# Products with v in threes directly ahead of scores, one queue at both ends, own places for six score blocks

## The chip, the cores and the metric

The kernel runs on one core of a Trainium2 chip. Such a core has five engines, each with its own instruction stream: TensorE (PE) multiplies matrices, VectorE (DVE), ScalarE (ACT) and GpSimd (POOL) work on elements, and SyncE (SP) issues most of the transfers (DMA). They wait for one another by semaphores. The metric is the time of one execution on the device, in microseconds (us); smaller is better.

## The reference

Two batches of 12 heads, 448 positions, head size 64, pass through attention with mixed heads, then through two mixing networks, all in float32:

```python
scores = scale * np.matmul(q, k.transpose(0, 1, 3, 2))
scores = np.einsum('bhij,hg->bgij', scores, w_pre)     # mixes the heads
attn = softmax(scores)                                 # row by row
attn = np.einsum('bhij,hg->bgij', attn, w_post)        # mixes the heads again
x = np.matmul(attn, v)                                 # to (batch, position, 768)
h = np.maximum(xt @ w_tok1, 0.0) @ w_tok2              # over positions, xt = x transposed
u = x + h transposed
x = u + np.maximum(u @ w_ch1, 0.0) @ w_ch2             # over channels
# then a gated network: gelu(x @ w_in), halves u and v, v normalised and mixed
# over positions, out = x + (u * v) @ w_out
```

## The kernel before

Attention works on chunks of queries: 120, 120, 120 and 88 of the 448 of a batch (`CH`, line 48), eight chunks in all. For a chunk, `qk` (line 348) multiplies queries and keys for a pair of heads at a time; the two heads lie in the two halves of the partitions, so that each matmul uses 64 rows of the array and two run side by side. In the first batch a product is taken in float32, in the second in three products of parts (high times high, high times low, low times high). The scores of a chunk are copied to SBUF, tile `S`, heads beside positions.

Ten queries of a chunk with their 12 heads make a block of 120 partitions. A block is a DMA from `S` to a tile `P` (`b_dma`, line 382), so that heads come to lie on partitions and can be mixed by a matmul. There are 90 blocks: 12, 12, 12 and 9 for the chunks of a batch. The loop at line 568 takes one step for each, and every step works at several distances: it starts the DMA of block i + 8 (`LD`), splits block i + 6 (`LS`) into a high part `Ph` on ACT and a low part `Pl` on POOL or DVE, mixes heads and takes the exponential of block i + 4 (`b_pre`, `LP`), and normalises. For block i itself `b_post` mixes the heads again in four matmuls, and `b_turn` copies that to the tile `AT` of its chunk, on DVE, one step later. A pre is three matmuls (lines 412 to 414), a post is four (line 445, eight instructions). Both use the whole array.

Two more kinds of work stand between these steps. Scores of the chunk after next come in three steps of every chunk, two pairs of heads in each, by a table `extra` from step to work (lines 535 to 553). `av` (line 456) multiplies a finished chunk's `AT` with v for one pair of heads; its outputs are 64 columns wide, and two run side by side. When av is due is told by `av_due` (line 557): up to the last step with scores (`LAST`, step 70) three in step 2 and three in step 6 of a chunk of 12 blocks (3 and 7 of a chunk of 9), later two at a time. The banks of PSUM for scores and av come from one pool of three (`psA`); every second pair of scores takes one of its two from `psC`.

Tiles `P` come from a ring of `NP_BUFS` = 4; the first two blocks have places of their own among the tiles for the keys of the second batch. The engines run their instructions in the order in which the program writes them (line 987).

From step 71 on the weights of the later networks are loaded, and converted by a generator of steps on ACT, DVE and POOL: `pump(n)` (line 175) runs n of them, `rounds(n, w)` (line 188) runs waiting follow-up work n times and w conversion steps with each.

Of the kernel before, what the change touches and what calls it, by code (L numbers as in the profile page):

```python
# [8 lines left out]
F32 = mybir.dt.float32  # L9
# [21 lines left out]
def tile_kernel(ctx, tc, q, k, v, w_pre, w_post, w_tok1, w_tok2, w_ch1, w_ch2,  # L31
                w_u, w_v, g_ln, w_sg, b_sg, w_out, out):
    nc = tc.nc
    B, D, H, S = 2, 64, 12, 448
    P = 128
    R = 4
    KP = S // R
    NP = H // 2
    C = H * D
    NCC = C // P  # L40
# [5 lines left out]
    IB = 10  # L46
    BW = IB * H
# [18 lines left out]
    xT = xpool.tile([P, NCC, T], F32, name="xT")  # L66
# [108 lines left out]
    def pump(n):  # L175

        for _ in range(n):
            if wstate["conv"] < wstate["room"]:
                next(wstate["steps"], None)
# [8 lines left out]
    def rounds(n, w=1):  # L188

        for _ in range(n):  # L190
            for c in list(chains):
                if next(c, chains) is chains:
                    chains.remove(c)
            pump(w)
# [48 lines left out]
    for n, w in enumerate(chw):  # L243
        p_ch.append(piece(w, P, NCC, P))
        if n in V_EARLY:
            j = V_EARLY[n]
# [3 lines left out]
    for o in GATE_ORDER.split():  # L250
        j = int(o[1])
# [94 lines left out]
    SS = {}  # L346
# [34 lines left out]

    def b_dma(i):
        b, c, j, (r0, stp, m) = blocks[i]
        if i < 2:

            t = qp.tile([P, S], F32, tag=f"KH{NP - 1 - i}", name=f"P{i}")[:BW]
        else:
            t = ap_.tile([BW, S], F32, tag="P", name=f"P{i}", bufs=NP_BUFS)
        src = SS[b, c][r0:r0 + (m - 1) * stp + 1:stp]
        if i == 0:  # L390

            for eng, r in ((nc.sync, slice(0, IB // 2)), (nc.scalar, slice(IB // 2, IB))):
                eng.dma_start(out=t[r.start * H:r.stop * H], in_=src[r])
        else:
            nc.sync.dma_start(out=t, in_=src)
        st[i]["P"] = t

    def b_high(i):
# [91 lines left out]
    chunks = [(b, c) for b in range(B) for c in range(len(CH))]  # L490
    NCH = len(chunks)
    LAST = 0


    load_k(0, 0)
# [39 lines left out]
    for x in range(2, NCH):  # L535
        b, c = chunks[x]
        n_prev = len(chunk_blocks(CH[chunks[x - 1][1]][1]))
        f0 = first[chunks[x - 1]] - LD
        nxt = chunks[x + 1] if x + 1 < NCH else None
        nxt2 = chunks[x + 2] if x + 2 < NCH else None  # L540
        for i in range(NP):

            s_ = f0 + 1 + i // 2 * n_prev // (NP // 2)
            LAST = max(LAST, s_)
            if i % 2:
                add(s_, qk, b, c, i, ((psA, "A"), (psC, "C")), (nc.scalar.copy, nc.vector.tensor_copy))
            else:
                add(s_, qk, b, c, i)
            if nxt and i % QG == QG - 1:
                if x > 3:  # L550
                    add(s_ + 3, qprep, *nxt, i // QG)
                if nxt2:
                    add(s_ + 4, load_q, *nxt2, i // QG)

    todo = []

    def av_due():
        if i > LAST:
            return todo and NP - len(todo) < 2 * ((j + nb // 6) * 3 // nb)

        at = (2, 6) if nb == 12 else (3, 7)
        return todo and NP - len(todo) < 3 * sum(j >= a for a in at)

    NS = S // KP
    X, RX = {}, {}
# [2 lines left out]
    for i in range(-LD, NB):  # L568
# [25 lines left out]
        if i >= 0:  # L594
            b, c, j, bl = blocks[i]
            b_post(i)
            if i >= NB - LP:
                b_turn(i)

            nb = len(chunk_blocks(CH[c][1]))  # L600
            if i > LAST + 3 and av_due():

                pump(4)
            while av_due():
                av(*todo[0])
                if todo[0][1] == len(CH) - 1 and b:
                    add(i + 1, load_v, b, todo[0][2])
                todo.pop(0)
            if j == nb - 1:
                todo = [(b, c, hp) for hp in range(NP)]  # L610
        if i == LAST:
# [39 lines left out]
    def bs(b):  # L651
        return slice(b * S, (b + 1) * S)
# [18 lines left out]
    with ExitStack() as mctx:  # L671
# [22 lines left out]
        def tok2(b):  # L694
            rh, rl, got = RR[b]
            finish(*got)
            t2 = [p for i in p_t2 for p in parts(i)]
            for cc in range(NCC):
                cs = slice(cc * P, (cc + 1) * P)
                ps = bank(f"t2ps{b}_{cc}")  # L700
                mm3(ps[:, :S], [((rh[:, tt, cs], rl[:, tt, cs]), t2[tt]) for tt in range(TOK // P)])
                U[cc, b] = later(add_split(cc, b, ps[:, :S], uh, ul))
                rounds(2, 0)

        X[1] = [mp.tile([KP, NS, C], F32R, name=f"x{nm}1") for nm in "hl"]
        RX[1] = [mp.tile([P, TOK // P, C], F32R, name=f"r{nm}1") for nm in "hl"]
# [192 lines left out]
    for cc, b in [(0, 0), (1, 0), (0, 1), (1, 1)] + [(cc, b) for cc in range(2, NCC) for b in range(B)]:  # L899
        finish(*[G[b, d] for d in range(ND)])  # L900
        need(p_o[cc])
        wo = parts(p_o[cc])
        ps = bank(f"ops{b}_{cc}")
        mm3(ps[:, :S], [(wo[d], (gh[:, d, bs(b)], glo[:, d, bs(b)])) for d in range(ND)])
        nc.vector.tensor_tensor(xT[:, cc, bs(b)], ps[:, :S], xT[:, cc, bs(b)], op=ALU.add)
        if cc == NCC - 1 and b == B - 1:
            for eng, r in ((nc.sync, slice(0, P // 2)), (nc.scalar, slice(P // 2, P))):
                eng.dma_start(out=out[r, cc, b], in_=xT[r, cc, bs(b)])
        else:
            nc.sync.dma_start(out=out[:, cc, b], in_=xT[:, cc, bs(b)])  # L910
        if b == B - 1:
            used()
        rounds(2, 2)
# [90 lines left out]
```

## Time and profile before

| | |
|---|---|
| median of 3 runs | 547.39 us (547.05 to 548.63) |
| profiled execution | 548.4 us, span 545.7 us |
| granted clock of PE, mean | 0.999 of full speed |
| busy in the span | PE 98%, DVE 73%, ACT 50%, POOL 50% |
| chain that ended last | PE 90%, DVE 4%, DMA 2% |

The span runs from the first to the last instruction; the execution takes 2.7 us more. PE is nearly always busy, and the chain of work that ended last is nearly all PE. A busy PE is not a PE at its peak: a matmul is busy from its first to its last column, and those that follow begin before it ends. Attention takes the span's first 227 us, of which the first 28 are a start-up in which the engines wait for one another and for transfers; the two networks behind it take the rest.

### The profile page before, as it was taken

To read this page: it belongs to the slowest core of one execution; us is meant where nothing else is said; L and a number is where in the kernel's file an instruction comes from. 1 tells how busy PE (TensorE), PEld (TensorE's weight loads), DVE (VectorE), ACT (ScalarE), POOL (GpSimd) and SP (SyncE) were. 2 spreads that over 40 slices of the span, in tenths; PEclk is the share of its full clock that TensorE was granted. 3 is DMA by queue.
4 is the path that set the end of the run, shared out by engine and by line. 5 is a ranking of instruction groups with operands and counts; after the bars stand their busy time and mean duration, and the time that the engine had idled before them with its cause. 6 is when DMAs were issued, how large, how long until landed. Compare 5 with 4: busy or idle time off the path is not lost.

```text
span 545.7 us, 10049 instructions
## 1 busy us (share of the span) xinstructions
PE 535.9 (98%) x3612; PEld 475.4 (87%) x3612; DVE 396.2 (73%) x782; ACT 273.0 (50%) x580; POOL 273.1 (50%) x286
## 2 busy tenths in 40 slices
PE   8999999999999999999999999999999999999996
PEld 5678788898988888999999999999999998888986
DVE  4877776857767789685565768778887984898982
ACT  4776666857676756455433443433332343454410
POOL 0587887857676765027422332354444454057600
PEclk9999999999999999999999999999999999999999
DMA  6486234524422552131133443343453333102222
GB/s 203 171 239 208 97 119 100 138 83 142 156 102 91 176 157 69 61 115 59 58 117 97 127 139 120 104 150 113 119 171 96 102 103 124 39 1 60 96 101 102
DMA packets 26355, 63.11 MB, mean 116 GB/s; under 512 B 2930, under 2 KB 18850, under 8 KB 26306
## 3 DMA queue, kind: packets, MB, share of 16 engines
q1 hardware_dynamic: 25873, 61.88, 35.8%
q8 instruction: 29, 0.48, 0.4%
q10 hardware_dynamic: 433, 0.59, 0.3%
q14 instruction: 20, 0.16, 0.1%
HBM read 40.36 MB, written 2.75 MB: 79 GB/s over the span
## 4 chain that ended last, share of the span: by engine, by line
PE 90%; DVE 4%; DMA 2%; issue 2%; ACT 1%; POOL 0%; ACTq 0%; POOLq 0%; DVEq 0%
PE post L445 11%; PE qk L365 6%; PE av L463 6%; PE c2ps L644 5%; PE c1ps L644 5%; PE c1ps L643 5%; PE c2ps L643 5%; PE c1ps L645 5%; PE c2ps L645 5%; PE pre L412 4%; PE pre L414 3%; PE pre L413 3%; PE ups L643 2%; PE ups L645 2%; PE ups L644 2%; PE vps L644 2%
## 5 line engine op out<-in xcount | busy, mean ns | idle before, releaser
L406 POOL TENSOR_TENSOR Pl<-P,Ph 120x448 fp32r<-120x448 f32 x87 | 100.3, 1153 | 62.4 <-ACT Ph L400 47.8
L162 POOL TENSOR_TENSOR wl<-cv,wh 128x768 fp32r<-128x768 f32 x28 | 52.6, 1880 | 119.5 <-ACT wh L161 81.2
L445 PEld LDWEIGHTS post<-wt,E 120*112 120x112 f32 x720 | 86.2, 176 | 4.9 <-POOL wt L433 0.5
L445 PE MATMUL post<-wt,E 120*112 120x120 f32 x720 | 88.7, 266 | 0.0
L420 ACT ACTIVATE E<-pre,nm 120x448 f32<-120x448 f32 x90 | 57.3, 636 | 43.4 <-DVE rc L427 38.9
L453 DVE COPY AT<-post 112x480 f32<-112x480 f32 x90 | 58.8, 653 | 6.3 <-PE post L445 0.3
L416 DVE TENSOR_REDUCE nm<-pre 120x1 f32<-120x448 f32 x90 | 55.0, 611 | 5.8 <-PE pre L414 3.8
L139 DVE SCALAR_TENSOR_TENSOR cv<-raw,cv 128x768 uint32<-128x768 uint32 (+3 forms) x44 | 54.1, 1229 | 1.3
L400 ACT CAST Ph<-P 120x448 fp32r<-120x448 f32 x90 | 51.7, 577 | 5.0 <-DMA P<-S 5.0
L644 PE MATMUL c2ps<-r1l,wh 128*128 128x448 f32 x144 | 52.9, 367 | 0.0
L644 PE MATMUL c1ps<-ul,wh 128*128 128x448 f32 x144 | 52.9, 367 | 0.0
L643 PE MATMUL c1ps<-uh,wh 128*128 128x448 f32 x144 | 52.3, 363 | 0.0
L643 PE MATMUL c2ps<-r1h,wh 128*128 128x448 f32 x144 | 52.3, 363 | 0.0
L645 PE MATMUL c1ps<-uh,wl 128*128 128x448 f32 x144 | 52.0, 361 | 0.0
L645 PE MATMUL c2ps<-r1h,wl 128*128 128x448 f32 x144 | 52.0, 361 | 0.0
L117 ACT ACTIVATE cv<-raw 128x768 f32<-128x768 f32 (+3 forms) x44 | 36.2, 823 | 26.7 <-POOL wl L162 19.2
L141 DVE SCALAR_TENSOR_TENSOR cv<-raw,cv 128x768 uint32<-128x768 uint32 (+3 forms) x44 | 41.3, 938 | 1.1
L412 PE MATMUL pre<-Ph,wpl 120*120 120x448 f32 x90 | 40.4, 449 | 1.1 <-DVE rc L427 0.9
L161 ACT CAST wh<-cv 128x768 fp32r<-128x768 f32 x28 | 23.4, 837 | 35.1 <-DVE cv L141 33.0
L463 PE MATMUL av<-AT,vn 112*64 112x120 f32 (+1 forms) x768 | 40.7, 262 | 0.0
L463 PEld LDWEIGHTS av<-AT,vn 112*64 112x64 f32 x768 | 37.0, 137 | 2.1 <-issue 0.2
L433 POOL TENSOR_SCALAR wt<-wd_post,rr 120x120 f32<-120x120 f32 x90 | 36.1, 401 | 4.5 <-DVE rr L430 1.7
(202 smaller groups left out, 1182.1 us busy)
## 6 DMA issues: line engine op xcount, KB each, us to landing
P<-S SPq DMA_DIRECT2D x89, 210.0 KB
raw<-in_w_ch_dram SPq DMA_DIRECT2D x24, 768.0 KB
raw<-in_w_v_dram SPq DMA_DIRECT2D x6, 512.0 KB
raw<-in_w_u_dram SPq DMA_DIRECT2D x4, 768.0 KB
raw<-in_w_out_dram SPq DMA_DIRECT2D x6, 512.0 KB
vn<-in_v_dram SPq DMA_DIRECT2D x12, 224.0 KB
out_dram<-xT SPq DMA_DIRECT2D x11, 224.0 KB
qn<-in_q_dram SPq DMA_DIRECT2D x10, 180.0 KB
```

Of the source, the lines that this page charges most:

```text
L139: nc.vector.scalar_tensor_tensor(fi, lo, 29, fi, op0=ALU.logical_shift_right, op1=ALU.bitwise_or)
L162: nc.gpsimd.tensor_tensor(dst[1], f, f32(dst[0]), op=ALU.subtract)
L406: eng.tensor_tensor(lo, st[i]["P"], f32(st[i]["h"]), op=ALU.subtract)
L412: nc.tensor.matmul(ps[:BW, :S], lhsT=wpl, rhs=hi, start=True, stop=False)
L416: nc.vector.tensor_reduce(out=nm, in_=ps[:BW, :S], axis=AX.X, op=ALU.max, negate=True)
L420: nc.scalar.activation(e, ps[:BW, :S], AF.Exp, bias=nm, scale=1.0, accum_out=sm)
L445: nc.tensor.matmul(ps[:KP, r * BW:(r + 1) * BW], lhsT=e[:, r * KP:(r + 1) * KP], rhs=wt, start=True, stop=True)
L453: nc.vector.tensor_copy(AT[b, c][:, :, :, j * IB:(j + 1) * IB], src)
L463: nc.tensor.matmul(ps[64 * j:64 * j + 64, :cols], lhsT=vn[b, hp][:, j, r, :], rhs=AT[b, c][:, r, 2 * hp + j, :cols], start=(r == 0), stop= ...
L643: nc.tensor.matmul(ps, lhsT=lh, rhs=rh, start=(start and i == 0), stop=False)
L644: nc.tensor.matmul(ps, lhsT=lh, rhs=rl, start=False, stop=False)
L645: nc.tensor.matmul(ps, lhsT=ll, rhs=rh, start=False, stop=(stop and i == n - 1))
```

## The change

Six edits. In `b_dma` six blocks, not two, get places of their own, and block 0 goes out as one DMA on SP, no longer in two halves on SP and ACT. The steps with scores are kept in a set. Up to `LAST`, av is due in the step just before one with scores, and in the last step of a chunk, three at a time; after it the rule for when is the old one. The conversions before av go three steps at a time, not four, with a single one at step 74. In the second token product every second output takes a conversion step. The last store goes out as one DMA.

```diff
     def b_dma(i):
         b, c, j, (r0, stp, m) = blocks[i]
-        if i < 2:
-            t = qp.tile([P, S], F32, tag=f"KH{NP - 1 - i}", name=f"P{i}")[:BW]
+        if i < NP:
+            t = qp.tile([P, S], F32, tag=f"K{'HL'[i % 2]}{NP - 1 - i // 2}", name=f"P{i}")[:BW]
         else:
             t = ap_.tile([BW, S], F32, tag="P", name=f"P{i}", bufs=NP_BUFS)
-        src = SS[b, c][r0:r0 + (m - 1) * stp + 1:stp]
-        if i == 0:
-            for eng, r in ((nc.sync, slice(0, IB // 2)), (nc.scalar, slice(IB // 2, IB))):
-                eng.dma_start(out=t[r.start * H:r.stop * H], in_=src[r])
-        else:
-            nc.sync.dma_start(out=t, in_=src)
+        nc.sync.dma_start(out=t, in_=SS[b, c][r0:r0 + (m - 1) * stp + 1:stp])
...
             s_ = f0 + 1 + i // 2 * n_prev // (NP // 2)
             LAST = max(LAST, s_)
+            scores.add(s_)
...
         if i > LAST:
             return todo and NP - len(todo) < 2 * ((j + nb // 6) * 3 // nb)
-        at = (2, 6) if nb == 12 else (3, 7)
-        return todo and NP - len(todo) < 3 * sum(j >= a for a in at)
+        return todo and (j == nb - 1 or len(todo) % 3 > 0 or i + 1 in scores)
...
             if i > LAST + 3 and av_due():
-                pump(4)
-            while av_due():
+                pump(3)
+            elif i == LAST + 4:
+                pump(1)
+            due = av_due()
+            while due:
                 av(*todo[0])
...
                 todo.pop(0)
+                due = av_due() and (i > LAST or len(todo) % 3)
...
                 U[cc, b] = later(add_split(cc, b, ps[:, :S], uh, ul))
-                rounds(2, 0)
+                rounds(1, cc % 2)
+                rounds(1, 0)
...
-        if cc == NCC - 1 and b == B - 1:
-            for eng, r in ((nc.sync, slice(0, P // 2)), (nc.scalar, slice(P // 2, P))):
-                eng.dma_start(out=out[r, cc, b], in_=xT[r, cc, bs(b)])
-        else:
-            nc.sync.dma_start(out=out[:, cc, b], in_=xT[:, cc, bs(b)])
+        nc.sync.dma_start(out=out[:, cc, b], in_=xT[:, cc, bs(b)])
```

On PE, around steps 12 to 14, the order was this (a number behind pre and post is the block; qk0_2 is batch 0, chunk 2, and behind it the head; av0_0 is batch 0, chunk 0, and behind it the pair of heads):

```order
L445 MATMUL post12_671<-wt12_621,E12_548 112x120 x4
L365 MATMUL qk0_2_8_695<-kn0_2_103,qn0_2_1_115 120x448
L365 MATMUL qk0_2_9_696<-kn0_2_103,qn0_2_1_115 120x448
L365 MATMUL qk0_2_10_701<-kn0_3_105,qn0_2_1_115 120x448
L365 MATMUL qk0_2_11_702<-kn0_3_105,qn0_2_1_115 120x448
L412 MATMUL pre17_707<-Ph17_625,wpl_70 120x448
...
L445 MATMUL post14_743<-wt14_676,E14_614 112x120 x4
L463 MATMUL av0_0_0_748<-AT0_0_310,vn0_0_383 64x120 x8
L463 MATMUL av0_0_1_758<-AT0_0_310,vn0_1_411 64x120 x8
L463 MATMUL av0_0_2_768<-AT0_0_310,vn0_2_439 64x120 x8
L412 MATMUL pre19_795<-Ph19_680,wpl_70 120x448
```

and is now this (pre and post have the lines 406 and 439, av has 457):

```order
L439 MATMUL post12_670<-wt12_620,E12_547 112x120 x4
L457 MATMUL av0_0_0_675<-AT0_0_309,vn0_0_382 64x120 x8
L457 MATMUL av0_0_1_685<-AT0_0_309,vn0_1_410 64x120 x8
L457 MATMUL av0_0_2_695<-AT0_0_309,vn0_2_438 64x120 x8
L365 MATMUL qk0_2_8_724<-kn0_2_103,qn0_2_1_115 120x448
L365 MATMUL qk0_2_9_725<-kn0_2_103,qn0_2_1_115 120x448
L365 MATMUL qk0_2_10_730<-kn0_3_105,qn0_2_1_115 120x448
L365 MATMUL qk0_2_11_731<-kn0_3_105,qn0_2_1_115 120x448
L406 MATMUL pre17_736<-Ph17_624,wpl_70 120x448
```

The three av moved from behind post 14 to behind post 12, in front of the scores. Eleven groups of three stand so in the whole program, behind the posts 12, 16, 24, 28, 37, 41, 45, 49, 57, 61 and 69; before, ten groups of three and six of two stood apart from scores.

On ACT, at the end of attention, the first conversion (L117, absolute value, tile `cv0`) stood ahead of av's copy (E is the exponential of a block, Ph its high part):

```order
L420 ACTIVATE E78_3008,pre78_3002<-pre78_3002,nm78_3006 120x448
L400 CAST Ph81_3019<-P81_2963 120x448
L420 ACTIVATE E79_3034,pre79_3028<-pre79_3028,nm79_3032 120x448
L117 ACTIVATE cv0_3041<-raw0_2933 112x512
L468 COPY xT_66<-av1_1_2_3046 128x12x10
```

and now stands a step earlier:

```order
L414 ACTIVATE E78_3017,pre78_3011<-pre78_3011,nm78_3015 120x448
L117 ACTIVATE cv0_3024<-raw0_2942 112x512
L394 CAST Ph81_3030<-P81_2972 120x448
L414 ACTIVATE E79_3045,pre79_3039<-pre79_3039,nm79_3043 120x448
L394 CAST Ph82_3071<-P82_3000 120x448
```

It moved past one exponential and one cast; the three DVE operations that read `cv0` stand behind the same reduction (of block 79) as before.

## Rows read from the trace of the kernel before

**Rows 1.** Busy time by stage: window, length, then busy time of each engine.

```profile
28.40:193.00 164.60, 164.60 (x1530) 142.17 (x1531) 117.87 (x342) 113.28 (x294) 123.43 (x164) 1.00 0.44 138
193.00:227.20 34.20, 32.87 (x388) 29.25 (x386) 30.86 (x83) 18.95 (x51) 16.09 (x21) 1.00 0.33 102
```

**Rows 2.** Order of time, PE: start, duration, engine, line, operation, count.

```profile
48.79 0.98 PE L445 MATMUL post<-wt,E 120*112 120x120 f32 x8
49.70 2.68 PE L463 MATMUL av<-AT,vn 112*64 112x120 f32 x48
52.31 0.46 PE L412 MATMUL pre<-Ph,wpl 120*120 120x448 f32 x1
...
53.03 0.98 PE L445 MATMUL post<-wt,E 120*112 120x120 f32 x8
53.77 0.44 PE L412 MATMUL pre<-Ph,wpl 120*120 120x448 f32 x1
...
54.45 0.98 PE L445 MATMUL post<-wt,E 120*112 120x120 f32 x8
55.36 1.74 PE L365 MATMUL qk<-kn,qn 64*88 64x448 f32 x8
```

**Rows 3.** The same, step 71: two products with v.

```profile
182.78 1.86 PE L463 MATMUL av<-AT,vn 112*64 112x120 f32 x32
184.57 0.46 PE L412 MATMUL pre<-Ph,wpl 120*120 120x448 f32 x1
```

**Rows 4.** The same, step 5: four pairs of score matmuls.

```profile
29.70 1.77 PE L365 MATMUL qk<-kn,qn 64*120 64x448 f32 x8
31.40 0.47 PE L412 MATMUL pre<-Ph,wpl 120*120 120x448 f32 x1
```

**Rows 5.** Order of time, all engines, start-up; in brackets idle time and releaser.

```profile
10.54 0.91 SPq L393 DMA_DIRECT2D P<-S  x1
10.55 1.72 ACTq L393 DMA_DIRECT2D P<-S  x1
...
12.90 2.52 PE L365 MATMUL qk<-kn,qn 64*120 64x448 f32 x12 [0.87 <-ACT S L368]
...
15.35 0.82 PE L512 MATMUL idle<-ident 128*128 128x128 f32 x5
```

**Rows 6.** Order of time, DVE, then PE, step 12.

```profile
43.64 0.66 DVE L453 COPY AT<-post 112x480 f32<-112x480 f32 x1
...
44.96 0.64 PE L365 MATMUL qk<-kn,qn 64*120 64x448 f32 x2
```

**Rows 7.** Order of time, SP, 16 to 20 us.

```profile
18.84 0.77 SPq L395 DMA_DIRECT2D P<-S  x1
```

**Rows 8.** Order of time, ACT and PE, block 8.

```profile
26.50 0.57 ACT L400 CAST Ph<-P 120x448 fp32r<-120x448 f32 x1 [1.20 <-DMA P<-S]
...
27.45 0.37 PE L413 MATMUL pre<-Ph,wph 120*120 120x448 f32 x1
...
28.35 0.47 PE L414 MATMUL pre<-Pl,wph 120*120 120x448 f32 x1 [0.54 <-POOL Pl L406]
```

**Rows 9.** Order of time, DVE and PE, steps 75 to 77.

```profile
191.81 0.43 DVE L135 TENSOR_SCALAR cv<-cv 112x512 f32<-112x512 f32 x1 [1.39 <-ACT cv L117]
...
194.67 0.44 PE L412 MATMUL pre<-Ph,wpl 120*120 120x448 f32 x1 [0.70 <-DVE rc L427]
```

**Rows 10.** Order of time, SP, the last two stores.

```profile
539.63 0.33 SPq L910 DMA_DIRECT2D out_dram<-xT  x1
542.05 0.59 SPq L908 DMA_DIRECT2D out_dram<-xT  x1
```

**Rows 11.** By stage, as rows 1; the last two columns are DMA share and GB/s.

```profile
541.20:541.60 0.40, 0.17 (x1) 0.00 (x0) 0.20 (x1) 0.00 (x0) 0.00 (x0) 1.00 0.00 0
...
544.00:544.40 0.40, 0.00 (x0) 0.00 (x0) 0.00 (x0) 0.00 (x0) 0.00 (x0) 0.80 0.46 170
```

**Rows 12.** Order of time, ACT, step 13.

```profile
48.18 0.57 ACT L400 CAST Ph<-P 120x448 fp32r<-120x448 f32 x1 [2.18 <-DMA P<-S]
```

More of the change, by code (lines that the diff above doesn't have):

```diff
@@ L492, in tile_kernel @@
     LAST = 0
+    scores = set()
     load_k(0, 0)
```

## The prediction

> **What bounds the kernel now.** I read the busy time by stage first, then the order of time on TensorE (PE) through the attention stage, then what ended its waits, last the two ends of the span. In the attention stage PE is busy for the whole of 164.60 us, at a granted clock of 1.00 (2.4 GHz), and it is idle for 34.20 - 32.87 = 1.33 us in the 34 us in which attention runs out [rows 1]. A wait that goes elsewhere is therefore worth little; time comes only from PE's own stream, from the start-up before 28.4 us, from that 1.33 us, and from the end. "Busy" also hides something: a matmul that begins late leaves no gap where the one before it is still recorded as running. So I compare starts, not gaps. A step of the attention loop is "pre" (three products) and "post"; from the start of a post to the next pre are 53.77 - 53.03 = 0.74 us, and pre takes 54.45 - 53.77 = 0.68 us to the next post. When a post is followed by products with v ("av") or by scores ("qk"), the same post takes 49.70 - 48.79 = 0.91 us or 55.36 - 54.45 = 0.91 us: 0.17 us more. After av, pre takes 53.03 - 52.31 = 0.72 us: 0.04 more [rows 2]. Each group of av or qk thus pays on its way in and on its way out.
>
> **The change, part by part.**
>
> *Moving av ahead of qk.* Three av take 52.31 - 49.70 = 2.61 us [rows 2], two take 184.57 - 182.78 = 1.79 us [rows 3], so one is 0.82, three are 2.46, and 0.15 us of the group is entry and exit. For qk, six pairs of matmuls take 15.35 - 12.90 = 2.45 us [rows 5] and four take 31.40 - 29.70 = 1.70 us [rows 4]: 0.375 a pair, 1.50 for four, and 0.20 us around them. Apart, av costs 0.17 + 0.15 + 0.04 = 0.36 us beyond its products and qk 0.17 + 0.20 + 0.04 = 0.41 us, or 0.77 us for four changes of shape on the array, about 0.19 each. In the changed order eleven groups of three av stand directly before scores. Each such pair of groups has three changes: into av, from av to qk, out of qk. The change from av to qk stands nowhere in the trace of before. Its bounds: nothing (0.38 us is saved, 4.2 us in eleven) and as much as going out and in again (nothing is saved). I take one change like the others, 0.19 us, since av uses half the columns of the array and qk half the rows, so that the array is arranged anew there too. That saves 0.19 x 11 = **2.1 us**.
>
> The Trainium skill (TensorEngine Tiling (Array Packing), Key Properties) says that a change of the tiling mode, though not of the tile within a mode, drains TensorE. The rows agree that leaving the whole array costs, 0.17 us into av and as much into qk [rows 2]; no row shows one between two tiled modes. By that rule a third drain stays in every pair, and the sum is the one that I take.
>
> Can other engines follow? Every group of av moves earlier by two steps, none later, so at each step PE is where it was or later; no producer of pre or post has less time than before. What av itself needs has less. In five of the eleven places av now stands one step after the last block of its chunk, and needs VectorE's (DVE's) copy of that block. In the step where the first of them will stand the copy began at 43.64 and took 0.66 us, so it ends at 44.30, and PE was through with post at 44.96 [rows 6]: 0.66 us in hand. I charge nothing.
>
> *The start.* Block 0 went out in two halves, one on ScalarE's (ACT's) queue. ACT stood 1.72 us in that issue, its copies of scores waited behind it, and PE waited for them 0.87 us [rows 5]. On SP alone that wait goes: **0.87 us**, if the transfer comes no later. The half on SP took 0.91 us to issue [rows 5], a whole block later 0.77 us [rows 7], so SP is not held longer; PE makes scores until 15.35 [rows 5], and ACT needs block 0 only when these are copied. At worst half of the gain is lost. The Trainium skill (DMA: Bandwidth & Descriptors, Issuing engines are not separate DMA queues) holds that issuing from several engines at once saves only the sequencer's time to start the transfer. That would make a single queue the slower way; here the halves took longer to issue than a whole, and the measurement decides.
>
> Places of their own for six blocks instead of two: the ring of four places then begins with block 6, which need not wait until block 2 is used up. In before SP issued it only at 18.84 [rows 7]; six issues of about 0.8 us from 10.54 on would be over near 15.4. The consequence is seen at block 8, whose cast on ACT waited 1.20 us for a transfer, so that PE, which had begun the second product of that pre at 27.45, began the third at 28.35 [rows 8]: 0.90 us where a third of a pre, 0.68 / 3 = 0.23, is usual. With blocks 6 to 9 issued some 3 us earlier this goes: **0.67 us**. Next late would be GpSimd (POOL); if it is, I lose these 0.67 us again, not more. The six places are the tiles of the second half's keys, which are written from step 13 on; nobody waits for them.
>
> *Weight conversions at the end of attention.* The first absolute value (on ACT) now runs one step ahead of the three DVE operations that need it. In before DVE sat 1.39 us waiting for it, and with it all DVE work of the next step; PE waited 0.70 us for a reciprocal's input behind it [rows 9]. Now DVE begins 1.39 us earlier, while PE comes 0.82 us earlier too, since only one av stands there instead of two: 0.70 - 1.39 + 0.82 = 0.13 us is left, 0.57 us gained. Of the remaining 0.63 us of idle time in this stretch [rows 1] I count half, 0.3 us, because each later group loses one conversion step: **0.85 us**, between a loss of 0.3 and the 1.33 us that are there. The steps taken away here run in the second token product, six of them, beside PE.
>
> *The end.* The last store goes as a whole on one queue. Earlier ones like it: issued at 539.63 in 0.33 us, and no transfer runs from 541.20 on, 1.57 us later. The halves: issued at 542.05 in 0.59 us, and in 544.00 to 544.40 the queues were still 0.46 busy, so they end about 2.15 to 2.35 us after the issue [rows 10, 11]. **0.7 us** less, since nothing runs beside it. By the rule of the Trainium skill named at the start (DMA: Bandwidth & Descriptors, Issuing engines are not separate DMA queues), two halves would win half of a whole issue, 0.17 us, and the sum would be 4.3 us rather than 5.2; the rows show the opposite.
>
> Sum: 2.1 + 0.87 + 0.67 + 0.85 + 0.7 = 5.2 us. The profiled execution took 548.4 us (545.7 us of span and 2.7 us around it), so it would be 543.2; it lies 1.0 us above the median of 547.39, and against that the forecast is **542.2 us**.
>
> **Rivals.** (a) The change from av to qk is free, because both are tiled and their weights can be loaded beside running products: for it speaks that inside av two halves of the array run side by side without any loss; against it that av uses all rows and qk does not. Gain 3.1 + 4.2 = 7.3 us, 540.1 us. (b) Joining saves nothing: the change between two tiled shapes costs 0.38 us, as much as out and in. For it speaks that both entry costs are the larger part and may add up; against it nothing in the rows. Gain 3.1 us, 544.3 us. (c) Slower: scores directly after av need two of the three banks of PSUM that av has just filled, and their copies stand in ACT's queue behind a cast of a block. Such a cast has waited 2.18 us for its transfer [rows 12]; in before two steps lay between av and scores, now none, and PE would stand. If this falls on the five places of the first chunks, while keys and v are loaded, it costs 5 x 2.18 = 10.9 us: 553.1 us. It decides from 5.2 / 11 = 0.47 us a place on. Against it: the copies now stand before the next cast in ACT's order, and the first av is done 1.6 us before the scores. (d) That the order is not what the change says can be left out: the rows of PE's order show all eleven.
>
> **How the numbers follow.** Forecast 0.65, (a) 0.15, (b) 0.15, (c) 0.05. A difference of 0.3% (1.6 us) is what a measurement of this kernel can tell from none. (a) and (b) lie below 545.8 as well; the forecast fails to do so only if 3.6 of its 5.2 us are lost, for instance (b) together with the tail and one of the ends, for which I leave 0.07 of no change. Slower takes (c) less the part that is only eaten gain: 0.03. The range from 539.6 to 545.0 takes in (a) and (b) with half of the start lost; the likeliest case's own range is 541.2 to 543.4.
>
> **What the profile of the changed kernel shows if this is right.** A post before av still takes 0.91 us; from the last av to the end of qk there is about 0.2 us, not 0 or 0.4, beyond the products; PE is busy without a break from about 11 to 15 us and through block 8, so that the first scores of the third chunk begin near 28.2 instead of 29.70; DVE's first conversion has no wait of 1.39 us before it; the last store is over about 1.6 us after its issue. It would be wrong if PE waited for a copy of av or scores at the eleven places, if POOL became late in the six steps without av or scores after the last of them, or if block 0 arrived after ACT is through with its copies.

## The result, and the profile after

The changed kernel takes 542.74 us (median, 542.57 to 543.0) against 547.53 us of the kernel before in the same measurement (547.05 to 548.63): a ratio of 0.991, interval 0.9893 to 0.9927. The forecast was 542.2 us within 539.6 to 545.0. The profiled execution took 542.57 us with a span of 540.6 us; the span of before was 545.7. By the medians 4.8 us are saved, by the spans 5.1, where 5.2 were forecast. The sum came out; several of its terms did not.

To see where the 5.1 us of span went, I take the starts of marked matmuls on PE in both traces and subtract them stage by stage. These are worked out from the two traces, in us ("post 4" is the post of block 4; the last two lines are cut at the end of the last matmul):

```
stage on PE                                    before   after   change   forecast
start of the span to first pre (block 0)        16.50   15.64    -0.86     -0.87
first pre to post 4 (holds block 8's pre)       12.19   11.35    -0.84     -0.67
post 4 to post 69 (ten of the joined groups)   148.71  147.23    -1.48     -1.94
post 69 to first token product (tail, 11th)     49.87   48.20    -1.67     -1.04
both token products                             34.00   34.02    +0.02      0
first channel product                           87.36   88.18    +0.82      0
second channel product to output product       162.88  162.92    +0.04      0
output product to last matmul                   29.85   29.49    -0.36      0
last matmul to end of span                       4.34    3.56    -0.78     -0.7
```

(The forecast's 2.1 us of joining is split here as ten and one elevenths. "Tail" is from post 69 to the first token product.) The 0.36 us of the output product are no effect of the change: the same code took between 29.47 and 30.10 us in the runs below.

**Joined groups.** Order of time on PE in the kernel after, blocks 12 and 13 (start, duration, engine, line, operation, tile and shape, count); it answers to [rows 2]:

```profile
42.24 0.98 PE L439 MATMUL post<-wt,E 120*112 120x120 f32 x8
43.15 2.68 PE L457 MATMUL av<-AT,vn 112*64 112x120 f32 x48
45.77 1.77 PE L365 MATMUL qk<-kn,qn 64*120 64x448 f32 x8
47.46 0.46 PE L406 MATMUL pre<-Ph,wpl 120*120 120x448 f32 x1
```

Post before av still takes 43.15 - 42.24 = 0.91 us. Three av take 45.77 - 43.15 = 2.62 us although scores follow and not pre, as in [rows 2], where it was 2.61 us; and the scores after them take 47.46 - 45.77 = 1.69 us, as behind a post [rows 4]. So the change from av to scores is not free, and costs what any change costs as the prediction shares them out. What is saved at each place is one post that no longer pays 0.17 us and one pre that no longer pays 0.03: 0.194 us over all places, 2.13 us for eleven.

**Start.** Order of time, PE, and SP's queue; they answer to [rows 5, 7]:

```profile
9.51 5.05 PE L365 MATMUL qk<-kn,qn 64*120 64x448 f32 x26
14.49 1.16 PE L507 MATMUL idle<-ident 128*128 128x128 f32 x8
15.64 0.46 PE L406 MATMUL pre<-Ph,wpl 120*120 120x448 f32 x1
...
10.81 8.24 SPq L389 DMA_DIRECT2D P<-S  x10
```

The wait of 0.87 us inside the scores is gone; 26 matmuls run in one stretch. SP sends ten blocks in one stretch too.

**What PE waits for now.** The longest waits on PE in the kernel after, then three rows of the same view of the kernel before (engine, line, waiting for; total us, times, longest):

```profile
...
PE pre L408 <- POOL Pl L400: 1.0, 3, 0.6
PE c1ps L643 <- POOL ul L660: 0.5, 1, 0.5
...
```

```profile
...
PE pre L412 <- DVE rc L427: 0.9, 2, 0.7
PE qk L365 <- ACT S L368: 0.9, 1, 0.9
PE t1ps L643 <- DVE xT L471: 0.5, 1, 0.5
```

Three waits went or shrank: the one for ACT's copies of scores, that for the reciprocal's input at the tail (0.9 to 0.2 us), and one of 0.5 us of the first token product for DVE's copy of the last av, which the prediction had left out. New are the first channel product's wait for POOL and, within the 1.0 us of pre's waits for POOL, 0.28 us in the tail. The other new losses don't show as waits at all, since the matmul before is still recorded as running; they show in the starts.

**Loss 1: blocks 23 and 24.** Order of time, PE and then POOL, in the kernel after:

```profile
67.38 0.98 PE L439 MATMUL post<-wt,E 120*112 120x120 f32 x8
68.12 0.45 PE L406 MATMUL pre<-Ph,wpl 120*120 120x448 f32 x1
...
69.00 1.07 PE L439 MATMUL post<-wt,E 120*112 120x120 f32 x8
...
66.35 1.14 POOL L400 TENSOR_TENSOR Pl<-P,Ph 120x448 fp32r<-120x448 f32 x1
67.46 1.14 POOL L332 TENSOR_TENSOR KL<-kn,KH 128x448 fp32r<-128x448 f32 x1
68.58 0.36 POOL L427 TENSOR_SCALAR wt<-wd_post,rr 120x120 f32<-120x120 f32 x1
```

From the pre at 68.12 to the post at 69.00 are 0.88 us instead of 0.69: the post needs `wt`, which POOL finishes at 68.94, because a subtraction for the second half's keys (KL) stands before it. POOL needs 1.14 + 0.36 = 1.50 us for a block without KL; a bare step of PE, one without av or scores, takes 0.74 + 0.69 = 1.43 us. Joining made of two short breaks one long one, with runs of four bare steps in between, and in these POOL falls behind. Over the four starts from 69.00 to 71.59 us that is 0.19 + 0.09 + 0.07 + 0.09 = 0.44 us.

**Loss 2: the tail.** Order of time, PE, DVE, ACT and POOL, steps 75 to 78; they answer to [rows 9]:

```profile
187.90 1.04 PE L457 MATMUL av<-AT,vn 112*64 112x120 f32 x16
...
189.58 0.98 PE L439 MATMUL post<-wt,E 120*112 120x120 f32 x8
190.64 0.44 PE L406 MATMUL pre<-Ph,wpl 120*120 120x448 f32 x1
...
192.07 0.44 PE L406 MATMUL pre<-Ph,wpl 120*120 120x448 f32 x1
...
192.99 0.47 PE L408 MATMUL pre<-Pl,wph 120*120 120x448 f32 x1 [0.28 <-POOL Pl L400]
193.34 1.07 PE L439 MATMUL post<-wt,E 120*112 120x120 f32 x8
...
187.77 0.43 DVE L135 TENSOR_SCALAR cv<-cv 112x512 f32<-112x512 f32 x1
...
188.69 1.51 DVE L139 SCALAR_TENSOR_TENSOR cv<-raw,cv 112x512 uint32<-112x512 uint32 x1
...
190.34 0.16 DVE L421 TENSOR_SCALAR rc<-pre 120x1 f32<-120x1 f32 x1
...
191.15 0.56 ACT L394 CAST Ph<-P 120x448 fp32r<-120x448 f32 x1 [2.35 <-DMA P<-S]
...
191.79 1.15 POOL L400 TENSOR_TENSOR Pl<-P,Ph 120x448 fp32r<-120x448 f32 x1 [1.35 <-ACT Ph L394]
```

The 1.39 us of DVE's waiting ahead of L135 are gone, as forecast. But the reciprocal's input (L421) still stands behind the conversions, and from the post at 189.58 to the pre are 1.06 us where 0.74 is usual. Only one av stands there to cover it, because the eleventh joined group took three of the six. The larger loss is two starts later: from the pre at 192.07 to the post are 1.27 us where 0.69 is usual. The third product there waits for POOL's low part; POOL had waited 1.35 us for ACT's high part, and ACT 2.35 us for the block's transfer. In all eight traces here and below that have this tail with the eleventh group joined, the first stall is 0.32 to 0.34 us; the second is 0.5 to 0.9 us in six of them and 0.1 us or nothing in two. That is most of what makes this stage differ from run to run. In the four traces with the group apart neither stall is there. Why the transfer came late stays open.

In the kernel before, the same place on PE began so (the pre that follows, at 194.67, stands in [rows 9]):

```profile
192.99 0.98 PE L445 MATMUL post<-wt,E 120*112 120x120 f32 x8
```

By starts it took 194.67 - 192.99 = 1.68 us, 0.94 more than usual.

**Loss 3: the first channel product.** It multiplies the high and low parts of the token mixer's result (`uh`, `ul`) with those of the weights (`wh`, `wl`); POOL makes both low parts. Order of time, PE, then POOL, then DVE:

```profile
263.12 0.37 PE L642 MATMUL c1ps<-uh,wh 128*128 128x448 f32 x1
264.03 0.47 PE L643 MATMUL c1ps<-ul,wh 128*128 128x448 f32 x1 [0.55 <-POOL ul L660]
...
252.15 1.87 POOL L162 TENSOR_TENSOR wl<-cv,wh 128x768 fp32r<-128x768 f32 x1
...
256.95 7.03 POOL L660 TENSOR_TENSOR ul<-xT,uh 128x448 fp32r<-128x448 f32 x5
...
257.19 1.73 DVE L139 SCALAR_TENSOR_TENSOR cv<-raw,cv 128x768 uint32<-128x768 uint32 x1
```

From 263.12 to 264.03 are 0.91 us where 0.20 is usual. The last `ul` is over at 263.98; the conversion steps in the second token product have put a `wl` of 1.87 us between the `ul`, and five `ul` take 7.03 us, 1.41 each, while one takes 1.16 to 1.20 us when DVE does no conversion beside it.

**End.** Order of time, SP, and by stage (window, length, busy time of five engines, clock, DMA share, GB/s); they answer to [rows 10, 11]:

```profile
537.71 0.33 SPq L906 DMA_DIRECT2D out_dram<-xT  x1
```

```profile
539.40:539.80 0.40, 0.00 (x0) 0.00 (x0) 0.00 (x0) 0.00 (x0) 0.00 (x0) 1.00 0.00 0
```

The whole store is over before 539.40, at most 1.7 us after its issue.

### The profile page after: what moved, and what is told of

Same layout as the page of the kernel before. It is cut to its first block, busy times and chain, and to the rows that moved or that the text cites. A ratio compares the mean times of both kernels' runs of the same rounds, so it can differ in the third digit from the quotient of the medians.

```text
span 540.6 us, 10043 instructions
## 1 busy us (share of the span) xinstructions
PE 533.6 (99%) x3612; PEld 474.3 (88%) x3612; DVE 396.9 (73%) x782; ACT 274.1 (51%) x580; POOL 275.6 (51%) x286
## 4 chain that ended last, share of the span: by engine, by line
PE 89%; DVE 4%; POOL 4%; issue 1%; ACT 1%; DMA 1%; DVEq 0%; POOLq 0%; ACTq 0%
PE post L439 12%; PE qk L365 7%; PE av L457 6%; PE c2ps L643 5%; PE c2ps L642 5%; PE c2ps L644 5%; PE c1ps L643 5%; PE c1ps L644 5%; PE c1ps L642 5%; PE pre L406 4%; POOL ul L660 3%; PE pre L408 3%; PE pre L407 3%; PE ops L644 2%; PE ops L643 2%; PE ups L644 2%
## 5 line engine op out<-in xcount | busy, mean ns | idle before, releaser
L139 DVE SCALAR_TENSOR_TENSOR cv<-raw,cv 128x768 uint32<-128x768 uint32 (+3 forms) x44 | 55.6, 1264 | 1.3
L117 ACT ACTIVATE cv<-raw 128x768 f32<-128x768 f32 (+3 forms) x44 | 36.2, 824 | 24.6 <-POOL wl L162 17.3
L141 DVE SCALAR_TENSOR_TENSOR cv<-raw,cv 128x768 uint32<-128x768 uint32 (+3 forms) x44 | 40.9, 930 | 1.0
```

The source lines that it names most:

```text
L139: nc.vector.scalar_tensor_tensor(fi, lo, 29, fi, op0=ALU.logical_shift_right, op1=ALU.bitwise_or)
```

## The experiments

Twelve kernels, each with four or five timed runs. The medians of most of them differ by less than their intervals, so each verdict below rests on the stages of one trace each, which repeat within 0.1 us where nothing was touched. Three stages don't: the start, where the inputs' arrival moves all that follows by up to 1.3 us, the tail, and the output product (29.47 to 30.10 us).

```
kernel                      median us   ratio to before (interval)   span
changed kernel, again         542.81    0.9901 (0.9886-0.9916)       541.8
av apart                      543.70    0.9926 (0.9913-0.9940)       542.2
no steps in token product     543.75    0.9929 (0.9916-0.9942)       541.1
store in halves               543.95    0.9932 (0.9918-0.9945)       542.3
block 0 in halves             544.20    0.9939 (0.9926-0.9952)       542.7
two places                    542.76    0.9902 (0.9889-0.9916)       541.0
start all old                 544.13    0.9936 (0.9922-0.9950)       543.4
tail's steps old              543.09    0.9918 (0.9904-0.9932)       541.0
three mends                   542.58    0.9900 (0.9886-0.9914)       540.2
keys on VectorE               542.82    0.9908 (0.9892-0.9925)       542.4
keys in the breaks            540.47    0.9870 (0.9852-0.9888)       538.2
av in sixes                   541.09    0.9877 (0.9861-0.9893)       538.9
```

**The changed kernel again** (unaltered).

> The changed kernel once more, unaltered, as the yardstick for its neighbours on the same chip: 542.7 us (542.2 to 543.3), and by stages the same trace within 0.1 us, but for the arrival of block 0 at the start, which may differ by some tenths, and the last 14 blocks of attention.

Post 4 to post 69 took 147.19 us (147.23 in the first trace), the first channel product 88.14 (88.18), but the tail 48.97 instead of 48.20. Eight runs with the changed tail and the joined eleventh group gave 47.91 to 49.12 us, mean 48.4. The tail is therefore judged by means, and single tenths in it mean nothing.

**Products with v apart again.**

```
-        return todo and (j == nb - 1 or len(todo) % 3 > 0 or i + 1 in scores)
+        at = (2, 6) if nb == 12 else (3, 7)
+        return todo and NP - len(todo) < 3 * sum(j >= a for a in at)
...
-                due = av_due() and (i > LAST or len(todo) % 3)
+                due = av_due()
```

> The changed kernel with the products with v set apart from the scores again, as in the kernel before; the rest of the change stays. Theory: each of eleven joined groups saves one change of array shape, 0.194 us as read from the two traces (2.1 us), and the new order costs 0.44 us at blocks 23 and 24, where GpSimd comes late because four steps run without a break. Undone, the kernel takes 2.1 - 0.4 = 1.7 us more than the changed one: 544.4 us (543.8 to 545.0), post before av stays 0.91 us, and the stalls at 68 to 71 us are gone. Rival a (the change from av to scores is free): 0.38 x 11 - 0.4 = 3.8 us more, 546.5. Rival b (joining saves nothing): 0.4 us less, 542.3.

Post 4 to post 69 took 148.58 us: 1.4 more than in the changed kernel, and no stall at blocks 23 and 24. That agrees with ten changes saved less 0.44 (1.50), and excludes both rivals (3.8 - 0.4 and 0.4 the other way). The surprise is the tail, 47.57 us: 0.9 less than the mean with the joined group. PE in this kernel, where two av stand in the place of one:

```profile
189.45 1.86 PE L457 MATMUL av<-AT,vn 112*64 112x120 f32 x32
...
191.95 0.98 PE L439 MATMUL post<-wt,E 120*112 120x120 f32 x8
192.70 0.44 PE L406 MATMUL pre<-Ph,wpl 120*120 120x448 f32 x1
```

DVE does the same conversions at the same distance, L139 in 1.51 us again, but from post to pre are 192.70 - 191.95 = 0.75 us: the second av covers them. The late transfer's stall is not there either. So the eleventh joined group saves 0.19 us and loses more than 1 us. By these two stages the kernel loses 1.4 and gains 0.9, so joining is worth some 0.5 us as the change has it, and 1.7 was too much. The median, 0.9 to 1.0 us above the changed kernel's, lies just below the range that was expected; in the profiled execution the first pre began 0.8 us later, which is no effect of the edit.

**No conversion steps in the second token product.**

```
-                rounds(1, cc % 2)
-                rounds(1, 0)
+                rounds(2, 0)
```

> The changed kernel without the six conversion steps inside the second token product; they fall to the first channel product. Theory: these steps put VectorE operations and one more subtraction of 1.84 us on GpSimd into a stretch where GpSimd is nearly full, so its last subtraction of the token mixer's result ends late and the first channel product's second matmul starts 0.7 us late. Without them the first channel product is 0.8 us shorter: 541.9 us (541.6 to 542.3), with every such subtraction at 1.16 to 1.18 us. Rival: the wait belongs to the shorter distance between attention's end and the channel product, or it moves to the second piece of weights, which is now converted six steps later: no gain or a loss, 542.7 to 543.5, with a wait of PE for weights at the second group of the first channel product.

The theory missed, the rival was right: the first channel product took 88.51 us. All twelve `ul` took 1.16 to 1.20 us, as expected, and were done at 259.4, but PE waited for the next piece of weights instead (POOL, then PE):

```profile
245.97 13.43 POOL L660 TENSOR_TENSOR ul<-xT,uh 128x448 fp32r<-128x448 f32 x12 [2.63 <-ACT uh L658]
...
265.15 0.47 PE L644 MATMUL c1ps<-uh,wl 128*128 128x448 f32 x1 [0.88 <-POOL wl L162]
```

So some of the steps taken from the tail must run before PE needs that piece; neither none nor six of them in this stretch is free.

**The last store in halves; block 0 in halves; two places; both edits of the start undone.** These kernels restore lines of the kernel before, the fourth those of the second and the third:

```
store:    for eng, r in ((nc.sync, slice(0, P // 2)), (nc.scalar, slice(P // 2, P))): eng.dma_start(out=out[r, cc, b], ...)
block 0:  for eng, r in ((nc.sync, slice(0, IB // 2)), (nc.scalar, slice(IB // 2, IB))): eng.dma_start(out=t[...], in_=src[r])
places:   if i < 2: t = qp.tile([P, S], F32, tag=f"KH{NP - 1 - i}", ...)
```

> The changed kernel with the last store in two halves on two queues again. Theory: the halves take 0.59 us to issue and land 2.64 us after the issue began, the whole 0.33 and 1.92 us, so 0.7 us more: 543.45 us (543.1 to 543.8). Rival (two issuing engines save issue time, as the Trainium skill, DMA: Bandwidth & Descriptors, Issuing engines are not separate DMA queues, has it): half an issue less, 542.6.

From the last matmul to the end are 4.31 us, against 3.56: 0.75 more, as forecast, and no half issue is won. (The median, 543.95 us, is above the expected range, which ended at 543.8; the tail of the profiled execution took 49.12 us.) Each half is longer to issue than the whole (SP and ACT):

```profile
538.70 0.58 SPq L908 DMA_DIRECT2D out_dram<-xT  x1
...
538.71 0.56 ACTq L908 DMA_DIRECT2D out_dram<-xT  x1
```

> The changed kernel with block 0 sent in two halves, one on ScalarE's queue, again; places of their own for six blocks stay. Theory: ScalarE stands 1.7 us in its issue and TensorE waits for its copies of scores for 0.87 us: 543.6 us (543.3 to 543.9), and the first pre (block 0) begins 0.87 us later. Rival: the start is set by the arrival of block 0 and not by ScalarE, so PE would only have less filler: 542.7.

The wait is back (PE, scores of the second chunk):

```profile
13.60 2.52 PE L365 MATMUL qk<-kn,qn 64*120 64x448 f32 x12 [0.79 <-ACT S L368]
...
17.20 0.47 PE L412 MATMUL pre<-Ph,wpl 120*120 120x448 f32 x1
```

The first pre began at 17.20, 1.56 us later than in the changed kernel, but part of that is arrival of inputs: the copies of scores ahead of the issue were already late. From the start of ACT's last copy ahead of that place to its first cast of a block are 4.94 us in all runs with a whole block 0 and 5.99 to 6.08 in the three with halves (the kernel before among them). Halves cost 1.05 to 1.14 us, which is more than expected, and the median, 544.20 us, lies above the range that ended at 543.9. The single difference of 0.86 in the table above is 1.14, less 0.28 us by which the inputs came later.

> The changed kernel with places of their own for two blocks instead of six; block 0 still goes out whole on one queue. Theory: block 6 is sent only when block 2's place is free, blocks 6 to 8 come 2 to 3 us later, the cast of block 8 waits and TensorE loses 0.9 us once in that block: 543.6 us (543.3 to 544.0), all of the loss between the first pre and post 8. Rival: in the changed kernel the transfers run earlier anyway, since nothing waits for ScalarE at the start, and two places do: 542.7.

The theory was wrong, the rival right: first pre to post 4 took 11.35 us as in the changed kernel, and block 8 does not stall.

> The changed kernel with both edits of the start undone: block 0 in halves on two queues and places of their own for two blocks. Each of them undone alone left block 8 without a stall (post 4 begins 11.35 us after the first pre in both). Theory: the stall of block 8 needs both, since the transfers of blocks 6 to 8 come too late only when the ring makes them wait and ScalarE is late as well; with both undone it is there again: 12.2 us from the first pre to post 4 as in the kernel before, and the first pre comes about 1 us later than with a whole block 0. Sum 1.9 us more than the changed kernel: 544.7 us (544.1 to 545.3). Rival: the joined groups or another part of the change already removed that stall: 11.35 us, and 543.8.

As expected: 12.15 us, and the third product of block 8's pre waits again (PE):

```profile
29.32 0.47 PE L414 MATMUL pre<-Pl,wph 120*120 120x448 f32 x1 [0.49 <-POOL Pl L406]
```

So the stall of block 8 needed both, block 0 in halves and a ring from block 2 on. With block 0 whole, own places are worth nothing; with own places, halves cost 1.1 us but no second stall.

**The tail's conversion steps as before** (four ahead of each late group, none in the token product).

```
-                pump(3)
-            elif i == LAST + 4:
-                pump(1)
+                pump(4)
...
-                rounds(1, cc % 2)
-                rounds(1, 0)
+                rounds(2, 0)
```

> The changed kernel with the conversion steps of the weights at attention's end as before: four before each late group of av, no single one ahead, and none in the second token product. The joined groups and the rest of the change stay. Theory: VectorE waits again 1.4 us for the absolute value and TensorE loses about 1.4 us more between block 69 and the first token product than the changed kernel; the first channel product has no wait, 0.8 us less: 543.3 us (542.8 to 544.0). Rival: without the joined group at block 69 undone, GpSimd and not the conversions sets the end, so the end is as in the changed kernel and the sum is 541.9.

Tail 49.69 us, 1.2 more than the mean of 48.4; first channel product 87.36. The theory holds in both places: redistributing the steps is worth 1.2 us in the tail and costs 0.8 in the channel product.

**Three mends.**

```
-        return todo and (j == nb - 1 or len(todo) % 3 > 0 or i + 1 in scores)
+        return todo and (j == nb - 1 or len(todo) % 3 > 0 or i + 1 in scores and i + 1 < LAST)
-        add(13 + 2 * i, kprep, ...)
+        add((13, 14, 17, 18, 25, 26)[i], kprep, ...)
-        add(25 + 2 * g, qprep, 1, 0, g)
+        add(27 + 2 * g, qprep, 1, 0, g)
-                rounds(1, cc % 2)
+                rounds(1, cc % 2 * (1 - b))
```

> The changed kernel with three mends, each aimed at one loss that the traces showed. (1) The last of the eleven joined groups is set apart again, so that attention's end has a group of av after blocks 71, 75 and 79; (2) the preparation of the second half's keys stands in the steps 13, 14, 17, 18, 25, 26 and that of its first queries in 27 and 29, behind joined groups, instead of every second step from 13 to 27; (3) in the second token product the three conversion steps of the first half stay (they finish the second piece of weights for the first channel product) and the three of the second half go. Theory: GpSimd needs 1.15 + 0.36 = 1.51 us for a block and an unbroken step of TensorE lasts 1.43 us, so GpSimd catches up only beside av and scores, and joining took breaks away. Gains: (1) 0.6 us between block 69 and the first token product, (2) 0.4 us between blocks 22 and 26, (3) 0.8 us in the first channel product. Sum 1.8 us: 541.0 us (540.5 to 541.7). Rival for (3): the wait only moves to the next piece of weights, as it did without any step in the second token product, and the kernel keeps 542. Rival for (1): the stalls of the end are VectorE's conversions alone and stay: 541.6.

Two held: tail 47.41 us, first channel product 87.36 us. The second failed: the stall at 23 and 24 went, and three new ones of 0.6 to 0.7 us came at blocks 16, 20 and 28, so that the kernel won nothing in sum. POOL in this kernel, blocks 13 to 16:

```profile
47.48 1.14 POOL L332 TENSOR_TENSOR KL<-kn,KH 128x448 fp32r<-128x448 f32 x1
48.60 0.36 POOL L427 TENSOR_SCALAR wt<-wd_post,rr 120x120 f32<-120x120 f32 x1
50.02 1.14 POOL L400 TENSOR_TENSOR Pl<-P,Ph 120x448 fp32r<-120x448 f32 x1 [1.05 <-ACT Ph L394]
51.11 1.15 POOL L332 TENSOR_TENSOR KL<-kn,KH 128x448 fp32r<-128x448 f32 x1
```

POOL idles 1.05 us in the break, waiting for ACT's next high part, and the second KL stands behind that idle time. (ACT's cast stands behind an exponential that waited 0.88 us for DVE there. That three buffers for the high and low parts keep POOL from running further ahead, as was expected, is not shown.)

**Keys in the breaks.** As the kernel with three mends, but:

```
+        add((13, 13, 17, 17, 25, 29)[i], kprep, ...)
+        add(25 + 4 * g, qprep, 1, 0, g)
```

> As the kernel with three mends, but the preparation of the second half's keys stands in pairs in the same step (13, 13, 17, 17, then 25 and 29), and that of its first queries in 25 and 29. In the kernel with three mends the second subtraction of each pair stood one step later, behind the idle time of 1.0 to 1.5 us in which GpSimd waits for a free buffer after a break, and TensorE lost 0.6 us at each of blocks 16, 20 and 28. Theory: GpSimd cannot work ahead by more than its three buffers, so a break gives it time only for what stands in its order ahead of that wait; both subtractions there cost nothing. From post 4 to post 69 the kernel then takes 146.8 us, 0.44 less than the changed kernel, in place of 148.7; with the two mends that held (end of attention 47.4 us from post 69, first channel product 87.36 us) 540.3 us (539.8 to 541.0). Rival: it is VectorE's casts of the keys in pairs that delay the reciprocals, and the stalls at blocks 16, 20 and 28 stay: 542.2.

540.47 us (0.987, interval 0.9852 to 0.9888), the fastest of all: post 4 to post 69 in 146.83 us, tail 47.38, first channel product 87.36, each as forecast. Both KL now stand ahead of the idle time, and it is gone (POOL):

```profile
47.29 2.24 POOL L332 TENSOR_TENSOR KL<-kn,KH 128x448 fp32r<-128x448 f32 x2
49.52 0.36 POOL L427 TENSOR_SCALAR wt<-wd_post,rr 120x120 f32<-120x120 f32 x1
49.85 1.15 POOL L400 TENSOR_TENSOR Pl<-P,Ph 120x448 fp32r<-120x448 f32 x1
```

At blocks 16 and 20 DVE's casts of the keys stand closer together here than with three mends, so they are not the cause of the stalls there.

**Keys on VectorE.**

```
-        add(13 + 2 * i, kprep, 1, i, nc.vector.tensor_copy, nc.gpsimd)
+        add(13 + 2 * i, kprep, 1, i, nc.vector.tensor_copy, nc.vector if i > 3 else nc.gpsimd)
```

> The changed kernel with the subtractions of the last two key tiles of the second half (steps 21 and 23) on VectorE instead of GpSimd, in the same steps. Theory: GpSimd is what is late at blocks 23 and 24; with two subtractions of 1.14 us off its list the 0.44 us of stalls at 68 to 71 us go, and post 22 to post 26 takes 10.2 us instead of 10.62: 542.3 us. Rival: VectorE, which makes the reciprocals that GpSimd waits for, is the late one, and the stalls stay or grow: 542.8 or more.

Nearly nothing won: post 22 to post 26 took 10.55 us (10.63 in the changed kernel, 10.19 with the keys in the breaks). POOL is no longer late, but DVE is; its copy for av comes behind the moved subtraction (DVE, then POOL, then PE):

```profile
70.52 0.67 DVE L332 TENSOR_TENSOR KL<-kn,KH 128x448 fp32r<-128x448 f32 x1
...
71.70 0.64 DVE L447 COPY AT<-post 112x480 f32<-112x480 f32 x1
...
70.68 1.50 POOL L400 TENSOR_TENSOR Pl<-P,Ph 120x448 fp32r<-120x448 f32 x1
...
72.40 0.84 PE L457 MATMUL av<-AT,vn 112*64 112x120 f32 x12 [0.28 <-DVE AT L447]
```

Here another place in the order won what another engine did not. (A stall of 0.26 us at block 12 in this run, ahead of the edit, I did not follow.)

**All six av together.** As the kernel with the keys in the breaks, and:

```
-                due = av_due() and (i > LAST or len(todo) % 3)
+                due = av_due() or (todo and i < 69)
```

> As the kernel with the keys prepared in the breaks, with joining driven further: all six products with v of a chunk stand together ahead of the chunk's first scores, instead of three and three. Five groups of av less stand by themselves ahead of scores, so five entries into av are saved (0.15 to 0.19 us each, 0.75 to 0.95 us). Theory: breaks of scores alone last 1.9 us, GpSimd falls behind by only 0.08 us a step, and outside the stretch where keys and queries are prepared it has 0.5 us in hand at each fourth step: the saving stays there, and is lost at the queries and keys: 0.5 us less in sum than without this step. Rival: GpSimd, which loses every second long break, is late at each fourth step, or the copies of six products stop TensorE at three banks: 1 us or more slower.

Post 4 to post 69 took 146.56 us, 0.27 less: 0.59 us of stalls at blocks 19 to 20 and 31 to 32 (POOL late again) are in it, so the five changes saved some 0.86 us, 0.17 each. The copies of six products stop nobody: the six take 5.07 us, 6 x 0.82 + 0.15 by the prices of [rows 2, 3]. The profiled execution is 0.8 us longer than that of the kernel with the keys in the breaks, as its first pre began 1.07 us later, in code that is the same; the medians differ by 0.6 us in the same direction. I count it as no clear gain.

## Why the prediction was right, and where it was not

- *Joining, 2.1 us.* The unit was right, 0.194 us a place, because the change from av to scores costs a full change; rivals (a) and (b) fall by the starts in the trace and by the kernel with av apart. "I charge nothing" for the engines that follow was the failed step, and with it the reason that no producer of pre or post has less time than before. I looked at DVE's copy for av and not at POOL, which at 1.50 us a block is slower than a bare step of 1.43 and lives on the breaks; its lateness stood among the signs of being wrong, without a price. It took back 0.44 us at blocks 23 and 24. The eleventh group lost over 1 us in the tail: behind the conversions 0.32 us where 0.13 was expected, and 0.58 us (in this trace) at a pre whose block came late, which the prediction did not have. Rival (c) was not seen: no wait for banks or copies at the eleven places.
- *Start, 0.87 us.* Right in kind; the halves cost 1.05 to 1.14 us.
- *Block 8, 0.67 us.* It measured 0.84: the late third product also kept the next post, 28.70 - 28.35 = 0.35 us behind it instead of 0.20, which the 0.67 left out. The cause was half wrong: own places are enough, but so is a whole block 0, and the change has both.
- *Conversions at the end of attention, 0.85 us.* The mechanism (DVE no longer waits for ACT) was right, the size too small: with the eleventh group apart the tail falls from 49.87 to 47.4 us, about 2.4; as the change has it, to 48.4 on average. I had bounded it by the 1.33 us of idle time that are recorded there, against my own rule to compare starts: at the reciprocal alone 0.94 us were lost and not 0.70. I also read the stretch only to 227.2 us, and so missed that the first token product waited 0.5 us for DVE's last copy. Smaller delays went as well; with the old steps they are back, but their mechanism I did not follow.
- *"The six steps taken away here run in the second token product, beside PE."* Failed: 0.8 us. POOL was busy through that stretch, and every step there delays the last `ul`. The kernel without any and those with three show that both too many and too few cost, and that three are free.
- *Last store, 0.7 us.* Right: 0.75 to 0.78.

So 5.1 of 5.2 us of span came true with errors that cancel, and that they cancel is luck: block 8, the tail and the last store gave 0.9 more than forecast, the output product 0.4 by chance; the channel product and POOL's lateness took 1.3.

## What to carry to other kernels

Saving changes of array shape by joining groups is worth its 0.2 us each, but the groups were also the pauses in which a slower engine caught up: before joining, compare that engine's time per step with PE's bare step, and find what it must do in the long runs. An engine uses a pause only for work that stands in its order ahead of its next wait. Work moved "beside PE" is free only if the engines there have room, so read the busiest of them in the stretch that receives it.

## What the runs showed of the hardware that was not expected

- A change between two partial array shapes (112 x 64 weights to 64 x 120) is not free: three av take 2.61 to 2.62 us whether scores or a pre follow, and four pairs of scores 1.69 to 1.70 us whether av or a post stands before them. Shared out as in the prediction, that is about 0.19 us a change.
- DVE and POOL slow each other down. Beside DVE's conversions a `ul` on POOL took up to 1.87 us instead of 1.16, and L139 there took 1.73 us, 0.96 at most of its other places; a `Pl` took 1.50 us instead of 1.14 beside a subtraction on DVE. The same subtraction of 128 x 448 takes 0.67 us on DVE and 1.14 on POOL.
- Half a transfer is not half an issue: a half store took 0.56 to 0.58 us to issue on each of two queues, a whole one 0.33; half of block 0 held ACT for 1.64 to 1.72 us [rows 5], while SP sends ten whole blocks in 8.24 us.
